# Attention with a feed-forward branch on one core: head quads on four accumulator tiles, blocks taken in linear order, and GpSimd adds over up to three blocks

## The chip, the cores and the metric

The kernel runs on one core of one Trainium2 chip. A core has five engines with an instruction stream of their own each: TensorE (PE in the profile; its weight loads stand apart as PEld), VectorE (DVE), ScalarE (ACT), GpSimd (POOL) and SyncE (SP), which here issues most of the DMAs. The metric is the device time of one execution, in microseconds (us).

## The reference

For 2048 tokens of width 640, the input is normalised once, and two branches of it are added to the input: attention with 32 query heads of width 20 over a single key and value head, and a feed-forward network of width 1728 with a SiLU.

```python
def _A_ref(x, wq, wk, wv, wo):
    q = (x @ wq).reshape(B, S, H, Dh).transpose(0, 2, 1, 3)
    k = x @ wk
    v = x @ wv
    scores = jnp.einsum("bhqd,bkd->bhqk", q, k) * (Dh ** -0.5)
    p = softmax(scores, axis=-1)
    o = jnp.einsum("bhqk,bkd->bhqd", p, v)
    return o.transpose(0, 2, 1, 3).reshape(B, S, H * Dh) @ wo
def _B_ref(x, w1, w2):
    return jnp.einsum("bsf,fd->bsd", silu(jnp.einsum("bsd,df->bsf", x, w1)), w2)
xn = layernorm(x)
return x + _A_ref(xn, wq, wk, wv, wo) + _B_ref(xn, w1, w2)
```

## The kernel before

**Blocks, steps, groups.** The queries are cut into 4 chunks of 512, the keys into 16 tiles of 128. A *unit* is one head of one chunk, so there are 128. A *block* is one unit against one key tile: a score tile of 128 keys by 512 queries, one PSUM bank. There are 2048 blocks. Units are taken three at a time: 42 groups of three heads and one of two. A group runs over the 16 key tiles, and one key tile of one group is a *step*: 43 x 16 = 688 steps. A step computes its blocks' scores with one matmul each (L776, 32 rows of keys by 128 columns, three side by side in different row tiles of TensorE) into three of six banks; consecutive steps alternate between the two halves.

**Two kinds of exp.** ScalarE takes the exp of the step's first two blocks in one instruction of 1024 elements per partition (L794), or of all three (1536). In most steps the last block goes to VectorE instead: it clamps the scores to 16-bit integers (L808, array Z), whose bits, read as bf16, are a coarse exp. To make it finer, such a block is read three times with different offsets and scaled values: as it is (Z), with 43 added (Y, index 0) and with 86 added (Y, index 1). The first sum is made by VectorE for up to three blocks in one instruction (L878, 1536 elements), in `flush_z`; the second by GpSimd for one block in one instruction (L814, two 16-bit numbers handled as one 32-bit integer, so 256 elements), in `do_S`. `want_dve` says which steps give a block to VectorE: not the first 8, not the first step of a group (`KT_ACT`), not the last step of all, and none when the planner's estimate of VectorE's backlog is above 3.4 us (`DVE_TH`).

**The accumulator.** One PSUM bank, number 6, holds the products with the values (PV, L866, weights of 128 by 32). It has four column tiles of 32 partitions. The group's three heads have tiles 0, 1 and 2, with the normaliser as column 20 of the values. The second reading of a VectorE block goes to tile 3; the third goes wherever a tile is free, if need be split over the spare columns of tiles 0 and 1 (the "thirds", `emit_thirds`, `host`, and the instruction group named PT). PV instructions keep the order of their steps (`pv_wait`, `pv_q`); four matmuls in four tiles run side by side and form a *slot*. At a group's end (`end_group`) VectorE copies the bank to SBUF (L986), SP transposes it by DMA (L943), GpSimd puts the parts together in four instructions (L953, L956, L958), VectorE takes a reciprocal (L963), and GpSimd multiplies (L972). The next group's PV starts once the bank is copied.

**Other work.** Between scores and PV, PE takes *jobs* from the queue `misc`: projections of queries (L1064), the feed-forward matmuls (L1100 in, with a tanh on ScalarE at L1113 and a product on VectorE at L1118; L1168 out) and the attention's output matmuls (L1173). `fill_chunk` spreads each chunk's jobs over its steps. Small matmuls on zeros (L699, L712, "fill") occupy PE when the planner finds nothing to do.

**What sets the order.** The program is planned before it is built: `Sched.run` simulates the five engines with given durations and puts out a fixed order of instructions for each. `step` chooses for PE among the next scores, the next PV and a job. On the chip every engine keeps its order and waits on semaphores. The exp blocks live in a ring of 31 (E), the VectorE blocks in 4 sets of 3 (Z and Y).

**Before the first scores** the input is normalised and transposed, and keys and values are made; `PRO` is the order of that on PE. When group 0 ends, `late_loads` issues on SP the loads of w2 and wo and a 1 MB fill of the second query buffer, and on GpSimd five scalings of wo.

The lines on which blocks go to VectorE and when the first sum is made:

```python
if t < DVE_FROM or t % KT >= KT - NOD or t >= self.T - DVE_LAST or t % KT in KT_ACT:
    return False
...
if self.zblocks and (len(self.zblocks) >= (ZB if g < self.NG - 2 else 2) or t - self.zblocks[0][0] >= ZWAIT
                     or t == self.T - 1 or (kt == KT - 1 and g >= FLUSH_G)):
    self.flush_z()
```

Of the kernel before, what the change touches and what calls it, by code (L numbers as in the profile page):

```python
# [10 lines left out]
I32 = mybir.dt.int32  # L11
# [40 lines left out]
H0_STEP = 10  # L52
KT_ACT = (0,)
Y_POOL = True
Y_TIME = 0.72
Y_LOCK = False
# [8 lines left out]
PV_PRESS = 12  # L65
# [9 lines left out]
FLUSH_G = 0  # L75
NOD = 0
PV_HOLD = 11
# [6 lines left out]
PRO = "v0 t7 t8 v1 k2 k3 k4 q1 v2 d0 k5 k6 k7 v3"  # L84
# [6 lines left out]
class Op:  # L91
    __slots__ = ("eng", "dur", "fn", "deps", "prio", "seq", "end", "avail", "idx", "inc", "inc_no", "sem",
                 "on_sched", "name", "dma", "mode", "start", "mm", "work", "kt", "na", "rs", "re", "rl", "then", "after", "lock")

    def __init__(self, eng, dur, fn, deps, prio=0.0, name="", on_sched=None, mode=None):
        self.eng = eng
        self.dur = dur
        self.fn = fn
        self.deps = deps
        self.prio = prio  # L100
        self.name = name
        self.on_sched = on_sched
        self.mode = mode
        self.start = None
        self.end = None
        self.avail = None
        self.idx = None
        self.inc = False
        self.inc_no = None
        self.sem = None  # L110
        self.dma = False
        self.mm = 1
        self.work = dur
        self.then = None
        self.lock = False

# [5 lines left out]
class Sched:  # L122
# [139 lines left out]
    def emit(self):  # L262
        per = {e: [] for e in self.engs}
        for e in self.engs:
            seen = {}
            for op in self.order[e]:
                need = {}
                dm = {}
                for d in op.deps:
                    if d.dma:  # L270
# [90 lines left out]
class Builder:  # L361
# [17 lines left out]
    def alloc(self):  # L379
# [9 lines left out]
        self.v = sb([P, 5, KT, SLOT], BF16)  # L389
# [6 lines left out]
        self.stk = sb([P, 64], BF16)  # L396
        self.UT = sb([P, 2, 4, P], BF16)
        self.W = sb([P, 4, 3, DH + 1], F32)
# [4 lines left out]
        self.tb = sb([P, 2, QW], BF16)  # L403
        self.xres = sb([P, 4, D], BF16)
# [13 lines left out]
        self.rL = sb([P, 2, 4, 3], F32)  # L418
# [3 lines left out]
        self.c86 = sb([P, 1], I32)  # L422
# [28 lines left out]
    def steps_init(self):  # L451
        self.groups = []
        u = 0
        while u < NUNITS:
            self.groups.append(list(range(u, min(u + 3, NUNITS))))
            u += 3
        self.NG = len(self.groups)
        self.T = self.NG * KT
        self.s_next = 0
        self.pv_q = deque()  # L460
        self.pv_wait = deque()
        self.misc = deque()
        self.urgent = deque()
# [6 lines left out]
        self.group_dve = defaultdict(int)  # L470
        self.last_dve_kt = {}
        self.dve_steps = 0
        self.started = False
        self.pv_started = False
        self.u_open = False
# [4 lines left out]
        self.thirds = []  # L480
# [6 lines left out]
        self.first_step = {}  # L487
        for g, us in enumerate(self.groups):
            for x in us:
                self.first_step.setdefault(x // H, g * KT)  # L490
        self.first_step[QC] = self.T


    def more(self):
        return (self.s_next < self.T or bool(self.pv_q) or bool(self.misc) or bool(self.urgent)
                or self.cur_job is not None)
# [43 lines left out]
    def s_reads(self, t, dv):  # L540
        g, kt = divmod(t, KT)
        k = [("kT1" if dv else "kT", kt // 2), ("kT", kt // 2)]
        for x in self.groups[g]:
            k += self.qkeys(x // H, x % H)
            k.append(("qb", (x // H) % 2, x % H))
        return k
# [7 lines left out]
    def s_ready(self, t):  # L554
# [5 lines left out]
        nh = len(self.groups[t // KT])  # L560
# [10 lines left out]
    def step(self, now):  # L571
# [15 lines left out]
        pv_n = 0  # L587
        pv_r = INF
        for op in list(self.pv_q)[:4]:
            if not self.pv_started and not self.may_start_pv():  # L590
                break
            r = sc.ready(op)
            if op.kt < KT:
                r = max(r, self.reads_ready([("vv", op.kt // 2)]))
            if r <= now + 1e-9:
                pv_n += 1
            else:
                if pv_n == 0:
                    pv_r = r
                break  # L600
# [3 lines left out]
        if job is None:  # L604
            for q in (self.urgent, self.misc):
# [7 lines left out]
        used = sum(o.na for o in self.pv_q) + sum(o.na for o, _ in self.pv_wait)  # L613
        press = used > NBLK - PV_PRESS
        choice = None
        if pv_n and (self.pe_mode == "PV" or press or self.pv_q[0].mode == "M"):
# [3 lines left out]
        elif pv_n >= 2:  # L620
# [6 lines left out]
        if self.s_next >= self.T - LASTPV and pv_n:  # L627
            choice = "PV"
        if choice is None:
            return self.fill(now, min(nxt, limit)) or nxt  # L630
        if choice == "PV":
            head = self.pv_q[0]
            d = (0.216 if head.mode == "PV" else head.dur) + self.switch(head.mode)
# [4 lines left out]
        if choice == "PV":  # L638
            op = self.pv_q.popleft()
            if op.kt < KT:  # L640
                op.deps.add(sc.lastw[("vv", op.kt // 2)])
            op.dur = d
            op.work = min(op.work, 0.216)
            self.u_open = op.kt < KT - 1
            self.pe_mode = op.mode
            if op.kt == 0:
                self.u_last = []
            if op.kt == KT:
                self.u_last = op.after
            if op.kt == KT - 1 and getattr(op, "rl", None) is not None:  # L650
                self.u_last = [op.rl]
            if not self.pv_started:
                self.pv_started = True
                op.deps |= sc.deps_of((), [("B", UBANK)])
            sc.commit(op, now)
# [19 lines left out]
    def fill(self, now, until):  # L675
        if self.s_next >= self.T and not self.pv_q:
# [48 lines left out]
    def may_start_pv(self):  # L725
# [5 lines left out]
        return not self.pro_left or len(self.pv_q) >= PV_HOLD  # L731
# [14 lines left out]

    def want_dve(self, t):
        if t < DVE_FROM or t % KT >= KT - NOD or t >= self.T - DVE_LAST or t % KT in KT_ACT:
# [8 lines left out]
    def do_S(self, t, now):  # L757
        sc = self.sc
        g, kt = divmod(t, KT)
        us = self.groups[g]  # L760
        nh = len(us)
# [8 lines left out]
        def fn(pe):  # L770
            ins = None
            for j, x in enumerate(us):
                h = x % H
                r = (h % 4) * SLOT
                kk = 1 if (dv and j == nh - 1) else 0
                ins = pe.matmul(self.bk(par3 + j), self.kT[r:r + SLOT, kk, kt * P:(kt + 1) * P],  # L776
                                self.qT[r:r + SLOT, h // 4, (x // H) % 2, :],
# [20 lines left out]
        zs = zp = None  # L798
        gd = self.group_dve[g]
        if dv:  # L800
            self.dve_steps += 1
            self.group_dve[g] += 1
            self.last_dve_kt[g] = kt
# [7 lines left out]
            self.y_on_pool = Y_POOL  # L811
            if self.y_on_pool:
                c86 = bass.AP(self.c86, self.c86[:, :].offset, [list(self.c86[:, :].ap[0]), [0, QW // 2]])
                sc.new("pool", Y_TIME, lambda v: v.tensor_tensor(  # L814
                    self.Y[:, zs, 1, zp * QW:(zp + 1) * QW].bitcast(I32),
                    self.Z[:, zs, zp * QW:(zp + 1) * QW].bitcast(I32), c86, ALU.add),
                    [("Z", zs, zp), ("c86",)], [("Y", zs, 1, zp)], prio=4.0, name="yp").lock = Y_LOCK
        first = kt == 0
        last = kt == KT - 1

        if dv:
            y = self.Y[:, zs, 0, zp * QW:(zp + 1) * QW].bitcast(BF16)
            z = self.Z[:, zs, zp * QW:(zp + 1) * QW].bitcast(BF16)
        thirds = []

        def pfn(pe):
            ins = None
            for j in range(na):
                q = j if j < nh - 1 else 2
                ins = self.pv_mm(pe, q, 0, kt, self.E[:, (b0 + j) * QW:(b0 + j + 1) * QW], first, last)  # L830
            if dv:
                self.pv_mm(pe, 2, 0, kt, z, first, last)
                ins = self.pv_mm(pe, 3, 1, kt, y, gd == 0, False)
            if first and nh == 2:
                ins = self.pv_mm(pe, 1, 0, kt, self.zero[:, 0:QW], True, False)
            for x in thirds:
                ins = x(pe, 3)
            return ins
        pv = sc.new("pe", 0.3, pfn, [("E", b0 + j) for j in range(na)], [("UB",)],
                    name=f"PV{t}", mode="PV", queue=False)  # L840
        pv.after = None if dv or nh < 3 or gd == 0 else thirds
        pv.mm = na + (2 if dv else 0) + (1 if first and nh == 2 else 0)
        pv.kt = kt
        self.pv_last = pv
        pv.na = na
        self.pv_wait.append((pv, dv))
        if self.thirds and self.can_host(pv):
            self.host(pv, self.thirds.pop(0))
        if dv:
            self.zblocks.append((t, pv))  # L850
        if self.zblocks and (len(self.zblocks) >= (ZB if g < self.NG - 2 else 2) or t - self.zblocks[0][0] >= ZWAIT
                             or t == self.T - 1 or (kt == KT - 1 and g >= FLUSH_G)):
            self.flush_z()
        elif last and self.thirds:
            self.emit_thirds([], None)
        self.move_pv()
        if last:
            self.end_group(g)

    def move_pv(self):  # L860
        waiting = set(id(p) for _, p in self.zblocks)
# [818 lines left out]
```

## Time and profile before

| | |
|---|---|
| median of 3 runs | 734.99 us (733.94 to 735.64) |
| span of the profiled execution (first to last instruction) | 732.1 us |
| granted TensorE clock | 0.997 |
| L794, exps of ScalarE | 688: 625 of 1024, 49 of 1536, 14 of 512 elements |
| L808, blocks of VectorE | 637, mean 684 ns |
| L878, first sums on VectorE | 218, mean 608 ns |
| L814, second sums on GpSimd | 637, mean 692 ns (least 602, median 611, most 1001) |
| L776, score matmuls | 2048 |
| L866, PV matmuls | 3534 |
| L986, evacuations of the accumulator | 43, mean 682 ns |
| first exp, last exp start | 16.9 us, 709.0 us |

The span is what the trace holds; the page gives no other time for the profiled execution, and the median of the runs lies 2.9 us above the span. The mean of an instruction is its own duration. Neighbours on one engine overlap, so what an instruction costs its engine is the distance from its start to the next start.

### The profile page before, as it was taken

The numbers are of one execution on the slowest core, as the hardware profiler recorded it, in microseconds if no ns is written. First come the engines' busy times: TensorE is split into PE (matmuls) and PEld (weight loads), VectorE is DVE, ScalarE is ACT, GpSimd is POOL, SyncE is SP. The second block draws the span as 40 slices with busy tenths as digits, with TensorE's granted clock in tenths as the row PEclk, the third lists the DMA queues.
The fourth block names the chain that finished last, engine by engine and source line by source line (L and its number), as shares of the span: only waits on it lengthen the run. The fifth ranks groups of instructions, "written<-read, shape, count | busy, mean of one in ns | idle before, by whom it ended". The sixth has DMA issues, their size and how long they took to land.

```text
span 732.1 us, 18886 instructions
## 1 busy us (share of the span) xinstructions
PE 714.9 (98%) x6863; PEld 229.2 (31%) x6863; DVE 652.6 (89%) x1189; ACT 695.8 (95%) x780; POOL 524.8 (72%) x897
## 2 busy tenths in 40 slices
PE   8898999999999999999999999999999999999998
PEld 4432222223333233222333233222233322322335
DVE  7788898998998999999899999999989899999883
ACT  6999999999999999999999999999999999999960
POOL 4376877677787777777777777767778877776770
PEclk9999999999999999999999999999999999999999
DMA  9546000000003011000102011110002001200011
GB/s 273 148 123 190 15 17 17 21 15 17 23 9 44 9 52 52 21 18 17 9 8 52 9 26 46 40 19 23 14 8 45 9 9 34 62 9 8 9 38 37
DMA packets 58546, 29.22 MB, mean 40 GB/s; under 512 B 44406, under 2 KB 57814, under 8 KB 58454
## 3 DMA queue, kind: packets, MB, share of 16 engines
q1 hardware_dynamic: 56998, 27.79, 15.1%
q8 instruction: 56, 0.92, 0.6%
q10 hardware_dynamic: 1456, 0.22, 0.2%
q14 instruction: 36, 0.29, 0.1%
HBM read 11.44 MB, written 2.62 MB: 19 GB/s over the span
## 4 chain that ended last, share of the span: by engine, by line
PE 70%; ACT 20%; issue 5%; DVE 4%; DMA 1%; POOL 1%; DVEq 0%; ACTq 0%; POOLq 0%
PE psall L866 23%; PE psall L776 22%; ACT sbt L794 18%; PE psall L1168 8%; PE psall L1100 7%; PE psall L1173 2%; PE psall L1064 2%; PE psall L712 2%; ACT sbt L1113 1%; DVE sbt L808 1%; PE psall L699 1%; DMA sbt<-sbt 1%; DVE sbt L1118 1%; ACT sbt L1458 1%; DVE sbt L1438 0%
## 5 line engine op out<-in xcount | busy, mean ns | idle before, releaser
L794 ACT ACTIVATE sbt<-psall 128x1024 bf16<-128x1024 f32 (+2 forms) x688 | 661.9, 1110 | 9.2 <-PE psall L776 7.7
L814 POOL TENSOR_TENSOR sbt<-sbt 128x256 int32<-128x256 int32 x637 | 436.8, 692 | 158.6 <-DVE sbt L808 143.9
L808 DVE TENSOR_SCALAR sbt<-psall 128x512 int16<-128x512 f32 x637 | 425.9, 684 | 48.2 <-PE psall L776 43.3
L776 PE MATMUL psall<-sbt 32*128 32x512 bf16 x2048 | 269.6, 385 | 6.4 <-ACT sbt L794 3.3
L866 PE MATMUL psall<-sbt 128*32 128x512 bf16 x3534 | 269.2, 385 | 2.1 <-POOL sbt L814 2.1
L776 PEld LDWEIGHTS psall<-sbt 32*128 32x128 bf16 x2048 | 69.2, 91 | 246.8 <-ACT sbt L794 81.1
L878 DVE TENSOR_SCALAR sbt<-sbt 128x1536 int16<-128x1536 int16 (+1 forms) x218 | 132.0, 608 | 2.0
L866 PEld LDWEIGHTS psall<-sbt 128*32 128x32 bf16 x3534 | 66.8, 94 | 113.7 <-issue 77.6
L1168 PE MATMUL psall<-sbt 128*128 128x320 bf16 x448 | 85.4, 302 | 0.2 <-DVE sbt L1118 0.2
L1100 PE MATMUL psall<-sbt 128*128 128x512 bf16 x260 | 79.9, 384 | 2.2 <-DVE sbt L1118 1.9
L1168 PEld LDWEIGHTS psall<-sbt 128*128 128x128 bf16 x448 | 34.7, 97 | 43.7 <-issue 33.1
L1118 DVE SCALAR_TENSOR_TENSOR sbt<-sbt,psall 128x512 bf16<-128x512 bf16 x54 | 36.8, 682 | 2.3 <-ACT sbt L1113 0.7
L1113 ACT ACTIVATE sbt<-psall 128x512 bf16<-128x512 f32 x54 | 37.1, 687 | 0.0
L986 DVE CAST sbt<-psall 128x512 bf16<-128x512 f32 x43 | 29.3, 682 | 1.7 <-PE psall L866 1.6
L1100 PEld LDWEIGHTS psall<-sbt 128*128 128x128 bf16 x260 | 17.8, 97 | 40.7 <-issue 25.8
L1064 PE MATMUL psall<-sbt 128*128 128x512 bf16 (+1 forms) x95 | 29.2, 385 | 0.4 <-DVE sbt L1118 0.4
L1173 PE MATMUL psall<-sbt 128*128 128x320 bf16 x144 | 29.0, 303 | 0.5 <-issue 0.4
L972 POOL TENSOR_TENSOR sbt<-sbt 128x240 bf16<-128x240 f32 (+2 forms) x44 | 25.4, 578 | 2.3 <-DMA sbt<-sbt 1.4
L958 POOL TENSOR_TENSOR sbt<-sbt 128x44 f32<-128x44 f32 x84 | 26.0, 309 | 1.1
L956 POOL CAST sbt<-sbt 128x168 f32<-128x168 bf16 x42 | 14.1, 335 | 9.0 <-DMA sbt<-sbt 9.0
L712 PE MATMUL psall<-sbt 128*128 128x512 bf16 (+1 forms) x70 | 17.4, 403 | 1.9 <-POOL sbt L1368 1.5
L1185 DVE SCALAR_TENSOR_TENSOR sbt<-psall,sbt 128x320 bf16<-128x320 f32 x28 | 13.6, 486 | 6.1 <-PE psall L1168 5.9
(88 smaller groups left out, 207.9 us busy)
## 6 DMA issues: line engine op xcount, KB each, us to landing
sbt<-in_A_x_dram SPq DMA_DIRECT2D x32, 160.0 KB, 3.3
out_dram<-sbt SPq DMA_DIRECT2D x15, 160.0 KB, 1.8
sbt<-in_B_w_dram SPq DMA_DIRECT2D x5, 432.0 KB, 6.6
sbt<-sbt SPq DMA_DIRECT2D x105, 20.0 KB
sbt<-in_B_w_dram SPq DMA_DIRECT2D x13, 160.0 KB, 2.9
sbt<-sbt SPq DMA_TRANSPOSE x68, 2.4
sbt<-sbt SPq DMA_DIRECT2D x1, 1024.0 KB, 6.1
sbt<-in_A_wo_dram SPq DMA_DIRECT2D x5, 160.0 KB, 2.7
```

The lines of the kernel that those rows point to most:

```text
L776: ins = pe.matmul(self.bk(par3 + j), self.kT[r:r + SLOT, kk, kt * P:(kt + 1) * P], self.qT[r:r + SLOT, h // 4, (x // H) % 2, :], start=Tru ...
L794: return a.activation(self.E[:, b0 * QW:(b0 + na) * QW], self.ps[:, par3 * BANK:(par3 + na) * BANK], AF.Exp, scale=ACT_SCALE)
L808: return v.tensor_scalar(self.Z[:, zs, zp * QW:(zp + 1) * QW], self.bk(bb), 0.0, ZMAX, ALU.max, ALU.min)
L814: sc.new("pool", Y_TIME, lambda v: v.tensor_tensor(self.Y[:, zs, 1, zp * QW:(zp + 1) * QW].bitcast(I32), self.Z[:, zs, zp * QW:(zp + 1) * ...
L866: return pe.matmul(self.bk(UBANK, 0, QW, q * SLOT, (q + 1) * SLOT), self.v[:, w, kt, :], x, start=start, stop=stop, tile_position=(0, q * ...
L878: sc.new("dve", Y_SLOW + t_dve_4x(w), lambda v, k=k: v.tensor_scalar(self.Y[:, zs, k, 0:n * QW], Z, float(PH[k + 1][0]), None, ALU.add), z ...
L1064: return pe.matmul(self.bk(b, 0, QW, 0, rows), self.wq[:, k, lo:hi], self.xnT[:, k, c * QW:(c + 1) * QW], start=(k == 0), stop=(k == DC - 1))
L1100: return pe.matmul(self.bk(b), self.w1[:, k, fk * P:(fk + 1) * P], self.xnT[:, k, c * QW:(c + 1) * QW], start=(k == 0), stop=(k == DC - 1))
L1113: sc.new("act", t_act(QW), lambda a: a.activation(t, src, AF.Tanh, scale=0.5), [("B", b)], [("tb", tp)], prio=X_PRIO, name=f"th{c}_{fk}")
L1118: sc.new("dve", t_dve_ps(QW), lambda v: v.scalar_tensor_tensor(out=self.hT[0:rows, fk, :], in0=t, scalar=1.0, in1=src, op0=ALU.add, op1=AL ...
L1168: return pe.matmul(self.bk(b, 0, 320), self.hT[r0:r1, fk, i * P:(i + 1) * P], self.w2[r0:r1, fk, e0:e0 + 320], start=(m == 0), stop=(m == ...
L1173: return pe.matmul(self.bk(b, 0, 320), self.oT[:, k, i * P:(i + 1) * P], self.wo[:, k, e0:e0 + 320], start=(m == 0 and src != "ps"), stop= ...
```

## The change

**Quads in linear order.** Groups are four heads of one chunk (32 groups). A group's 64 blocks are ordered by key tile, then head, and the 2048 blocks follow one another in one line; a step takes the next three, across key tiles and groups, so there are 683 steps, the last with two blocks.

**Head tiles.** Each head has its own column tile, and all three readings of a VectorE block are added there; the thirds and their splitting go, with the spare value columns and the merging on GpSimd. A reading is now an *item* in a queue of its group and tile (`tq`), and `do_pv` starts a slot with the first ready item of each of the four tiles. `pv_ready` counts how many full slots are ready; PV is chosen at `PV_GO` = 5, or with fewer if there is no job.

**GpSimd's adds** move from `do_S` to `flush_z`: one instruction over up to three blocks. The first sum may also be made there by GpSimd, when the planner finds that engine's queue shorter by a margin. **VectorE's steps**: excluded are the first 8, the last, and steps whose last block is one of the last two of its group; the rule on the first step of a group is gone. **Group end**: the DMA transpose takes all 128 rows, VectorE a reciprocal and GpSimd one product of 320 elements. The last group is transposed by four matmuls as a job and multiplied on VectorE.

**Prologue and constants**: `PRO` in another order and a queue of its own (`pro`), `H0_STEP` 14 for 10, `PV_PRESS` 8 for 12, `PV_HOLD` 29 exp blocks for 11 PV instructions; the query offset has its own tile (`qo`), and query jobs read the key `qz` (the fill of the query buffer).

```diff
-H0_STEP = 10
-KT_ACT = (0,)
-Y_TIME = 0.72
+H0_STEP = 14
-PV_PRESS = 12
+PV_PRESS = 8
-PV_HOLD = 11
+PV_HOLD = 29
-PRO = "v0 t7 t8 v1 k2 k3 k4 q1 v2 d0 k5 k6 k7 v3"
+NODB = 2
+GB = 4 * KT
+NB = NUNITS * KT
+Y0_POOL = 1.0
+Y0_COST = 1.45
+YP_FIX = 0.14
+YP_BLK = 0.47
+PV_MIN = 4
+PV_GO = 5
+PRO = "v0 t7 t8 v1 k2 k3 k4 k5 v2 k6 k7 v3 q1 d0"
...
+    def blocks(self, t):
+        return [(b // GB, b % GB // 4, b % 4) for b in range(3 * t, min(3 * t + 3, NB))]
...
+    def pv_ready(self, now):
+        if self.cg >= self.NG or (not self.pv_started and not self.may_start_pv()):
+            return 0, 0, INF
+        g = self.cg
+        closed = self.g_seen[g] == GB and not self.g_late[g]
+        most = max(len(q) for q in self.tq[g])
+        full, some, nxt = 99, 0, INF
+        for q in self.tq[g]:
+            n = 0
+            for it in q[:8]:
+                r = max(self.sc.ready(it), self.reads_ready([("vv", it.kt // 2)]))
+                if r <= now + 1e-9:
+                    n += 1
+                elif r < nxt:
+                    nxt = r
+            some += n > 0
+            if not closed or len(q) == most:
+                full = min(full, n)
+        if not self.sc_bank_free(now):
+            return 0, 0, nxt
+        return full, some, nxt
...
+    def do_pv(self, now, d):
...
+        for q in self.tq[g]:
+            for it in q[:8]:
+                if max(sc.ready(it), self.reads_ready([("vv", it.kt // 2)])) <= now + 1e-9:
+                    items.append(it)
+                    q.remove(it)
+                    break
...
     def want_dve(self, t):
-        if t < DVE_FROM or t % KT >= KT - NOD or t >= self.T - DVE_LAST or t % KT in KT_ACT:
+        g, kt, j = self.blocks(t)[-1]
+        if t < DVE_FROM or 4 * kt + j >= GB - NODB or t >= self.T - DVE_LAST:
             return False
...
+        if self.zblocks and (len(self.zblocks) >= ZB or t - self.zblocks[0][0] >= ZWAIT or t == self.T - 1
+                             or 3 * (t + 1) >= GB * (self.zblocks[0][1] + 1)):
             self.flush_z()
...
+        back = {e: max(sc.t[e], sc.t["pe"]) + sum(o.dur for o in sc.pend[e]) for e in ("dve", "pool")}
+        tp = YP_FIX + YP_BLK * n
+        td = Y_SLOW + t_dve_4x(w)
+        y0 = "pool" if back["pool"] + tp * Y0_COST < back["dve"] + td + Y0_POOL else "dve"
+        for k, e in ((0, y0), (1, "pool")):
+            yk = [("Y", zs, k, i) for i in range(n)]
+            if e == "dve":
+                sc.new("dve", td, lambda v, k=k: v.tensor_scalar(
+                    self.Y[:, zs, k, 0:w], self.Z[:, zs, 0:w], float(PH[k + 1][0]), None, ALU.add), zk, yk,
+                    prio=4.0, name=f"y{k}").lock = True
+                continue
+            c = self.cy[:, k:k + 1]
+            cb = bass.AP(self.cy, c.offset, [list(c.ap[0]), [0, w // 2]])
+            sc.new("pool", tp, lambda v, k=k, cb=cb: v.tensor_tensor(
+                self.Y[:, zs, k, 0:w].bitcast(I32), self.Z[:, zs, 0:w].bitcast(I32), cb, ALU.add), zk + [("cy",)], yk,
+                prio=4.0, name=f"yp{k}")
+        for i, (t, g, kt, j) in enumerate(self.zblocks):
+            for k in range(2):
+                self.item(g, j, kt, k + 1, lambda k=k, i=i: self.Y[:, zs, k, i * QW:(i + 1) * QW].bitcast(BF16),
+                          [("Y", zs, k, i)])
+            self.g_late[g] -= 1
...
+        op = sc.new(eng, 0.75 if eng == "pool" else t_dve_ps(16 * DH), lambda v: v.tensor_tensor(
+            dst, ut[:, :, :, 0:DH], rb, ALU.mult), [key, ("rL", up)], [("o", h0 + i) for i in range(4)],
+            prio=0.5 if eng == "pool" else U_PRIO, name=f"nrm{g}")
...
-        reads = [("xnT", 4 * c + i) for i in range(4)] + [("wqd", 0), ("wqd", 1)]
+        reads = [("xnT", 4 * c + i) for i in range(4)] + [("wqd", 0), ("wqd", 1), ("qz", c % 2)]
```

## The prediction

> **What bounds the kernel now.** I read the page's shares first, then its chain, then busy time by stage, then the groups by shape, and last the order of time on ScalarE and TensorE.
>
> ```profile
> span 732.1 us, 18886 instructions
> ...
> PE 714.9 (98%) x6863; PEld 229.2 (31%) x6863; DVE 652.6 (89%) x1189; ACT 695.8 (95%) x780; POOL 524.8 (72%) x897
> ...
> PE 70%; ACT 20%; issue 5%; DVE 4%; DMA 1%; POOL 1%; DVEq 0%; ACTq 0%; POOLq 0%
> ```
>
> Two engines look full, and the chain changes between them. The busy time by stage (columns: length, PE, PEld, DVE, ACT, POOL, clock, DMA share, GB/s) says which is full where:
>
> ```profile
> 16.86:38.00 21.14, 18.08 (x172) 9.00 (x170) 16.41 (x63) 20.46 (x22) 8.60 (x14) 1.00 0.65 172
> 200.00:400.00 200.00, 199.23 (x1977) 61.62 (x1973) 183.96 (x319) 199.57 (x218) 153.22 (x257) 1.00 0.12 25
> 695.90:710.00 14.10, 13.38 (x129) 3.92 (x126) 14.10 (x27) 10.62 (x17) 12.28 (x21) 1.00 0.23 49
> 710.00:732.10 22.10, 18.71 (x143) 11.36 (x141) 8.12 (x19) 1.60 (x5) 1.48 (x3) 0.99 0.09 30
> ```
>
> From the first exp at 16.86 to 695.9 ACT is never idle for long. In the last group, of two heads, it is idle for 3.5 of 14.1 us. In the tail PE works off output matmuls.
>
> ```profile
> L794 ACT ACTIVATE sbt<-psall 128x1024 bf16<-128x1024 f32 x625 | 594.5, 1090 | 4.9 <-PE psall L776 3.7 <-PE psall L866 0.4 <-ACT sbt L794 0.2
> L814 POOL TENSOR_TENSOR sbt<-sbt 128x256 int32<-128x256 int32 x637 | 436.8, 692 | 158.6 <-DVE sbt L808 143.9 <-PE psall L776 4.3 <-PE psall L866 2.1
> L878 DVE TENSOR_SCALAR sbt<-sbt 128x1536 int16<-128x1536 int16 x202 | 123.8, 614 | 1.9
> L794 ACT ACTIVATE sbt<-psall 128x1536 bf16<-128x1536 f32 x49 | 73.4, 1506 | 0.8 <-PE psall L776 0.8
> L972 POOL TENSOR_TENSOR sbt<-sbt 128x240 bf16<-128x240 f32 x40 | 23.9, 597 | 0.9 <-DVE sbt L963 0.6
> L953 POOL TENSOR_TENSOR sbt<-sbt 128x84 f32<-128x84 bf16 x42 | 15.1, 360 | 0.0
> L794 ACT ACTIVATE sbt<-psall 128x512 bf16<-128x512 f32 x14 | 8.3, 598 | 3.5 <-PE psall L776 3.2
> ```
>
> A mean of one (1090 ns) is not what an exp costs, because neighbours overlap. The cost is from start to start:
>
> ```profile
> 21.78 2.78 ACT L794 ACTIVATE sbt<-psall 128x1536 bf16<-128x1536 f32 x2
> 24.44 0.55 ACT L1412 ACTIVATE sbt<-sbt 128x400 bf16<-128x400 bf16 x1
> ...
> 310.27 3.81 ACT L794 ACTIVATE sbt<-psall 128x1024 bf16<-128x1024 f32 x4
> 313.88 0.69 ACT L1113 ACTIVATE sbt<-psall 128x512 bf16<-128x512 f32 x1
> 314.36 7.05 ACT L794 ACTIVATE sbt<-psall 128x1024 bf16<-128x1024 f32 x7
> ```
>
> So two blocks cost (313.88 - 310.27)/4 = 0.9025 us, three cost (24.44 - 21.78)/2 = 1.33, one of 512 costs 0.48. TensorE the same way:
>
> ```profile
> 309.33 0.39 PE L776 MATMUL psall<-sbt 32*128 32x512 bf16 x3
> 309.65 0.61 PE L866 MATMUL psall<-sbt 128*32 128x512 bf16 x8
> 310.20 0.39 PE L776 MATMUL psall<-sbt 32*128 32x512 bf16 x3
> ...
> 72.44 0.40 PE L866 MATMUL psall<-sbt 128*32 128x512 bf16 x4 [2.06 <-POOL sbt L814]
> ...
> 73.55 1.02 ACT L794 ACTIVATE sbt<-psall 128x1024 bf16<-128x1024 f32 x1 [2.04 <-PE psall L776]
> ```
>
> From the scores at 309.33 to the next PV at 309.65 are 0.32 us, and two PV slots reach the next scores at 310.20, 0.55 later: a slot takes about 0.22 and a change of kind 0.10 more. The pair at 72.44 and 73.55 shows the danger: when a PV at the head of PE's queue waits for a POOL add, ACT loses the same 2 us. Over the whole trace PV waited for that add only 16 times, 7.7 us.
>
> **The change, part by part.**
>
> *ScalarE's exps.* Before, 637 of 688 steps gave their last block to VectorE. The other 51 are the 43 first steps of a group, 7 more among the first 8, and the last; the backlog rule (3.4 us) never bit. Afterwards there are 2048/3 = 683 steps, and the excluded ones are the first 8, the last, and those whose last block is the 63rd or 64th of its 64 (21): 30. So 653 exps of two blocks, 29 of three, and the last step's two.
> Before: 625 x 0.9025 + 49 x 1.33 + 14 x 0.48 = 564.1 + 65.2 + 6.7 = 636.0.
> After: 654 x 0.9025 + 29 x 1.33 = 590.2 + 38.6 = 628.8. **-7.2 us**, on the engine that sets the pace. Each time the backlog rule bites costs 0.43 back.
>
> *The group of two heads* goes. Its idle 3.5 us (10.62 busy of 14.10) goes with it, since the last steps are now like the others: **-3.5**, if PE keeps up; 0 if not.
>
> *TensorE.* Five steps fewer: 5 x 0.32 = -1.6. PV: the starts of L866 cluster into 902 slots for 3534 matmuls. Afterwards each block gives one reading and each VectorE block two more, 2048 + 2 x 653 = 3354; by the rule of which tile gets the VectorE block, the fullest tile of each quad has 22 to 28, in sum 870 slots. That is 32 x 0.216 = -6.9 if every slot is full, and nothing if the planner starts slots half empty. I take half: PE needs some 5 us less where ACT needs 10.7 less. PE's room for the difference shows as fill matmuls, 47 on L699, about 10 us. I book **+1.5** for what PE can't follow (0 to +5).
>
> *GpSimd's adds.* 637 adds of one block become 221 of two or three (211 and 10, by the flush rule). No row shows 768 elements. From below: the rows of 84 and 240 elements rise by (597 - 360)/156 = 1.52 ns per element, so 692 + 512 x 1.52 = 1.47 us. From above: nothing saved, 3 x 692 = 2.08. Nearest is the same operation on 256, less the start of two, which those rows put at 360 - 84 x 1.52 = 0.23: 2.08 - 0.46 = 1.6. So 221 x 1.6 = 354 against 437.
> The Trainium skill (GPSIMD Engine Reference, section 3.1, Elementwise) says that a two-input operation costs about 2.6 cycles per element whatever its length, so that joining adds saves only their starts; an estimate from it, 768 x 2.6/1.2 GHz, is 1.66 us before the start, and by it the sum would be the same but the margin below thinner.
> Normalising: four rows (335, 360, 309 twice, and the 597) over 42 groups, 80 us, become 31 products of 320 elements, 0.597 + 80 x 0.00152 = 0.72 each: 22. POOL falls to 525 - 83 - 58 = 384, and takes those first-phase adds that the planner moves over from VectorE, 0 to 221 of 1.6 us; the rule sends one only where POOL's queue is the shorter, so I take a third, 74: about 500. It stays under the others.
>
> *VectorE.* 16 more reads of scores (426/637 = 0.67 each: +11), 11 fewer evacuations (0.68: -7.5), 74 fewer three-block adds (0.61: -45): about 611 of 653. Nothing on the path.
>
> *Handover of the accumulator.* PV of the next quad waits for the evacuation on VectorE, and behind it waits all later PV; scores and projections go on. One handover costs PV 2.3 us now (last PV ends at 302.57, next starts at 304.87). Afterwards there are 31 in place of 42, each up to 1 us longer, as the last add comes later (1.6 for 0.6): 31 x 3.3 = 102 against 42 x 2.3 = 97. Even. Its cover is the buffer of 31 exp blocks: a pause of 3.3 us fills about 7; without it, ACT would stand for 31 x 1 us.
>
> *Moved loads.* The end of group 0 moves from step 16 to step 22, some 6 us. With it, on SP's queue, go the transpose, 15 loads of w2 (8.5 us of issue from 50.78), 5 of wo, the 1 MB fill of the second query buffer, and on POOL the five scalings of wo (785 ns each). First users: the output matmuls at 166, and the second chunk's projections, which now wait for that fill ahead of PE's other jobs; they are paced past step 50. Nothing, unless such a job stands at the head early. The prologue's new order: ACT is busy 20.46 of 21.14 us there, so at best -0.7; I take 0, at worst +2.
>
> *Tail.* The last VectorE blocks' add is of two or three, so the last PV starts later by up to 1.6 - 0.6; the four transposing matmuls and the product of 320 in place of two of 80 add 0.1. PE has output matmuls to do meanwhile (it was busy 18.7 of 22.1), so I take **+1.0** (0 to +1.5).
>
> Sum: -7.2 - 3.5 + 1.5 + 1.0 = -8.2: a span of 723.9. The median of the runs, 734.99, lies 2.9 above this span; kept, that gives **727 us**, with 723 to 732 for this case.
>
> **The rivals.**
> 1. *PE follows less.* If slots go half empty, so that 902 stay, PE needs only 1.6 less; in the last chunk, where output matmuls are left over, that is what shows: 735 - 1.6 = **733**. For it: PE 98%, chain 70% PE. Against: fills exist, so PE had room.
> 2. *The adds come late (slower).* The planner counts 0.14 + 0.47 per block, 1.55 us for three; that is a number in the diff, not a measurement. If one really takes 2.08, each set is 0.53 late, and PE's order is fixed. If a quarter of the 221 is met at the head of PE's queue, 55 x 0.53 = 29 us; the room of 10 takes its part, 19 remain: 735 - 8.2 + 19 = **746**. For it: 72.44, and that the mean add, 692, lies above the median, 611, so POOL is already held up at times. Against: only 7.7 us of such waits now, though then with 0.72 planned for 0.69. It decides from 8.2 + 10 = 18.2 us, 0.33 in each of 55: at adds over 1.88 us.
> 3. *ACT gains all.* PE's room suffices and the tail hides its add: -10.7, and up to 4 more where 11 fewer handovers spare small waits of 0.3: **720 to 724**.
>
> **How the numbers follow.** Forecast 0.52; PE short 0.13; late adds 0.24; all gained 0.11. About 0.2% (1.5 us) is what a measurement of this kernel can tell from no change. Faster: 0.11, nearly all of 0.52, and a little of the PE case: 0.65. Same: 0.07, from the PE case. Slower: 0.24 and edges of the others: 0.28. The range 716 to 748 goes below the all-gained case by what its small waits may give, and above the late case's middle; some 0.15 stay outside.
>
> **What would show it.** Right: 653 exps of two blocks and 29 of three at the same spacing; ACT idle under 1 us per 100; last exp near 701; PV in some 870 to 890 slots; the three-block add near 1.6; the tail still 22 to 23. Wrong: PE's waits on POOL's adds above 20 us; more than 35 exps of three blocks (the backlog rule bites); the add above 1.9 us; POOL busier than 85%; or more output matmuls left after the last exp than now.

## The result and the profile after

The changed kernel takes 739.43 us (median of 4 runs, 738.85 to 740.91) against 735.07; the ratio is 1.0067, with a 95% interval of 1.005 to 1.0083. It is slower by 4.4 us where 8 us less were forecast. The profiled execution is the longest of the four, 740.91 us, 2.0 above its span.

From the page of the changed kernel, its shares and its chain:

```profile
span 738.9 us, 17791 instructions
...
PE 709.2 (96%) x6661; PEld 223.8 (30%) x6661; DVE 659.1 (89%) x1106; ACT 695.0 (94%) x775; POOL 489.8 (66%) x366
...
PE 58%; DVE 19%; issue 11%; POOL 8%; ACT 3%; DMA 0%; POOLq 0%; DVEq 0%
```

The chain is the work that ended last, followed back from the end. Before the change VectorE's share of it was 4%, GpSimd's 1% and "issue" (no wait that the profile shows) 5%; why issue rose to 11% is open. The span is longer, but ScalarE is busy for a smaller part of it (695.8 of 732.1 us before, now 695.0 of 738.9). The groups by shape (count, then busy us, mean ns, then idle time before them with what ended it) show what was counted rightly and what was not:

```profile
L841 ACT ACTIVATE sbt<-psall 128x1024 bf16<-128x1024 f32 x654 | 620.9, 1053 | 19.0 <-PE psall L823 15.9 <-ACT sbt L841 0.4
L856 DVE TENSOR_SCALAR sbt<-psall 128x512 int16<-128x512 f32 x653 | 433.2, 682 | 49.0 <-PE psall L823 41.5 <-POOL sbt L888 0.9
L888 POOL TENSOR_TENSOR sbt<-sbt 128x768 int32<-128x768 int32 x280 | 432.9, 1563 | 198.9 <-DVE sbt L856 155.3 <-PE psall L823 26.4 <-issue 4.1
L882 DVE TENSOR_SCALAR sbt<-sbt 128x1536 int16<-128x1536 int16 x142 | 123.8, 872 | 2.5
L841 ACT ACTIVATE sbt<-psall 128x1536 bf16<-128x1536 f32 x29 | 42.0, 1466 | 0.6 <-PE psall L823 0.5
```

The exps are the 653 + 1 and 29 that the rule gives. The joined GpSimd add takes 1.563 us. But VectorE's first sum on three blocks (now L882), the same instruction with the same shape as before, takes 872 ns in the mean, and took 614. VectorE stood idle for only 2.5 us before all 142 of them: the added time is inside the instruction.

The waits say who felt it. Before (waiter, awaited, us in total, times, longest):

```profile
PEld psall L776 <- DVE sbt L808: 45.2, 114, 1.0
...
ACT sbt L794 <- PE psall L776: 7.7, 15, 2.0
...
PEld psall L866 <- POOL sbt L814: 5.6, 15, 2.4
```

After:

```profile
PEld psall L823 <- DVE sbt L856: 71.2, 162, 1.2
...
ACT sbt L841 <- PE psall L823: 16.3, 35, 1.5
...
PEld psall L762 <- POOL sbt L888: 13.3, 43, 0.8
```

Scores (L823, in these rows by their weight loads, PEld) wait for a bank that VectorE has not read yet, 26 us more, and ScalarE waits for scores. The waits of PV (L762) on GpSimd grew as well, but only by 8 us.

**Where 6.8 us of span came from.** First exp at 18.0 in place of 16.9: +1.2. From the first exp's start to the last one's lie 692.2 us before and 701.6 after: +9.4; the exps need 7.2 less, so ScalarE's waits grew by 16.6 (3.8 of them before 60 us: idle 4.9 of 42.0 us there, 1.1 of 43.1 before). After the last exp's start 23.1 us remained, now 19.3: -3.8, since 42 feed-forward output matmuls are left over by then and 65 were before (23 x 0.136 us = 3.1); PE had had time for them while scores waited. Together 1.2 + 9.4 - 3.8 = 6.8.

**The clock is a small part.** The granted TensorE clock was 0.88 between 18.02 and 60 us and 1.00 in the same stage before. Over the span it was 0.992 (0.995 in the other three runs), before 0.997. An estimate from these: 0.005 of 738.9 us, some 4 us of TensorE's time at most in the profiled execution, and some 1.5 in the others.

The order of time shows one of the longest of ScalarE's waits, on four engines:

```profile
554.99 4.31 POOL L888 TENSOR_TENSOR sbt<-sbt 128x768 int32<-128x768 int32 x3 [0.95 <-PE psall L823]
...
558.02 1.69 DVE L882 TENSOR_SCALAR sbt<-sbt 128x1536 int16<-128x1536 int16 x1
...
560.04 1.95 DVE L856 TENSOR_SCALAR sbt<-psall 128x512 int16<-128x512 f32 x3
...
560.86 0.39 PE L823 MATMUL psall<-sbt 32*128 32x512 bf16 x3 [0.99 <-DVE sbt L856]
...
561.29 1.94 ACT L841 ACTIVATE sbt<-psall 128x1024 bf16<-128x1024 f32 x2 [1.54 <-PE psall L823]
```

GpSimd's adds run until 559.30. VectorE's sum starts at 558.02 and ends at 559.71, 0.41 after them. Behind it come one other VectorE instruction (0.48 us) and, at 560.04, the clamp of the next block; TensorE stands idle for 0.99 before the next scores, and ScalarE for 1.54. Sorted over the whole trace: VectorE's three-block sums that start while no GpSimd add runs take 563 ns in the mean (53 of them), those that start during one, at least 0.06 us before its end, 1056 (89). Before it was 558 (107) and 677 (95). Of the 89, 85 end 0.41 to 0.46 us after the very add that they met, and before 87 of the 95 did. So a sum that meets a GpSimd add stands until that ends, and an unhindered GpSimd add is now 1.46 us long where it was 0.61.

### The profile page after: what moved, and what is told of

Its sections match the earlier page's. It is cut to its first block, busy times and chain, and to the rows that moved or that the text cites. A ratio compares the mean times of both kernels' runs of the same rounds, so it can differ in the third digit from the quotient of the medians.

```text
span 738.9 us, 17791 instructions
## 1 busy us (share of the span) xinstructions
PE 709.2 (96%) x6661; PEld 223.8 (30%) x6661; DVE 659.1 (89%) x1106; ACT 695.0 (94%) x775; POOL 489.8 (66%) x366
## 4 chain that ended last, share of the span: by engine, by line
PE 58%; DVE 19%; issue 11%; POOL 8%; ACT 3%; DMA 0%; POOLq 0%; DVEq 0%
PE psall L823 19%; PE psall L762 18%; DVE sbt L856 11%; PE psall L1081 9%; POOL sbt L888 8%; PE psall L1013 5%; DVE sbt L882 5%; PE psall L977 2%; PE psall L684 2%; PE psall L1086 1%; ACT sbt L841 1%; DVE sbt L1031 1%; ACT sbt L1362 1%; DVE sbt L931 1%; DVE sbt L1116 1%
## 5 line engine op out<-in xcount | busy, mean ns | idle before, releaser
L841 ACT ACTIVATE sbt<-psall 128x1024 bf16<-128x1024 f32 (+1 forms) x683 | 658.1, 1071 | 19.7 <-PE psall L823 16.3
L888 POOL TENSOR_TENSOR sbt<-sbt 128x768 int32<-128x768 int32 (+1 forms) x292 | 446.6, 1546 | 202.2 <-DVE sbt L856 158.6
L856 DVE TENSOR_SCALAR sbt<-psall 128x512 int16<-128x512 f32 x653 | 433.2, 682 | 49.0 <-PE psall L823 41.5
L823 PE MATMUL psall<-sbt 32*128 32x512 bf16 x2048 | 268.2, 386 | 15.9 <-DVE sbt L856 10.9
L762 PE MATMUL psall<-sbt 128*32 128x512 bf16 x3354 | 263.8, 386 | 4.6 <-DVE sbt L931 2.3
L823 PEld LDWEIGHTS psall<-sbt 32*128 32x128 bf16 x2048 | 68.2, 91 | 255.6 <-issue 98.0
L882 DVE TENSOR_SCALAR sbt<-sbt 128x1536 int16<-128x1536 int16 (+1 forms) x150 | 131.5, 876 | 2.7
L762 PEld LDWEIGHTS psall<-sbt 128*32 128x32 bf16 x3354 | 65.0, 94 | 119.4 <-issue 76.0
L977 PE MATMUL psall<-sbt 128*128 128x512 bf16 (+1 forms) x95 | 28.9, 385 | 0.6 <-DVE sbt L1031 0.6
L920 POOL TENSOR_TENSOR sbt<-sbt 128x320 bf16<-128x320 bf16 x31 | 26.8, 865 | 3.8 <-DVE sbt L915 3.4
L931 DVE CAST sbt<-psall 128x512 bf16<-128x512 f32 x32 | 21.8, 680 | 2.1 <-PE psall L762 2.1
L684 PE MATMUL psall<-sbt 128*128 128x512 bf16 (+2 forms) x76 | 20.3, 420 | 1.5 <-POOL sbt L1281 1.5
L1482 POOL TENSOR_SCALAR sbt<-sbt 128x256 bf16<-128x256 bf16 x8 | 4.1, 514 | 23.4 <-DVE sbt L1480 23.3
L1098 DVE SCALAR_TENSOR_TENSOR sbt<-psall,sbt 128x320 bf16<-128x320 f32 x28 | 13.5, 484 | 4.6 <-PE psall L1081 4.2
L1116 DVE SCALAR_TENSOR_TENSOR sbt<-psall,sbt 128x320 bf16<-128x320 f32 x28 | 13.2, 480 | 3.1 <-PE psall L1086 3.1
```

The costliest lines, as they stand in the source:

```text
L684: return pe.matmul(self.bk(b, 0, n), self.zero[:, 0:P], self.zero[:, 0:n], start=True, stop=True)
L762: ins = pe.matmul(self.bk(UBANK, 0, QW, r, r + SLOT), self.v[:, it.w, it.kt, :], it.x(), start=f, stop=False, tile_position=(0, r), skip_g ...
L823: ins = pe.matmul(self.bk(par3 + i), self.kT[r:r + SLOT, kk, kt * P:(kt + 1) * P], self.qT[r:r + SLOT, g % 8, (g // 8) % 2, :], start=True ...
L841: return a.activation(self.E[:, b0 * QW:(b0 + na) * QW], self.ps[:, par3 * BANK:(par3 + na) * BANK], AF.Exp, scale=ACT_SCALE)
L856: return v.tensor_scalar(self.Z[:, zs, zp * QW:(zp + 1) * QW], self.bk(bb), 0.0, ZMAX, ALU.max, ALU.min)
L882: sc.new("dve", td, lambda v, k=k: v.tensor_scalar(self.Y[:, zs, k, 0:w], self.Z[:, zs, 0:w], float(PH[k + 1][0]), None, ALU.add), zk, yk, ...
```

## The experiments

Theory A is this hold. Rival B is the prediction's second rival, PV waiting for late GpSimd adds. Rival C is the other prologue and its clock. Times are medians; each ratio is against the kernel before on the same chip, whose medians lay at 734.2 to 734.4 (735.07 for the result above). Differences between two changed kernels are of their medians and so compare chips too.

**Short adds under the same plan.** In `flush_z`, the add's instruction is issued once per block. The planner's durations are untouched, so every engine keeps its order:

```diff
-            sc.new("pool", tp, lambda v, k=k, cb=cb: v.tensor_tensor(
-                self.Y[:, zs, k, 0:w].bitcast(I32), self.Z[:, zs, 0:w].bitcast(I32), cb, ALU.add), ...
...
+            def padd(v, k=k, c1=c1):
+                for i in range(n):
+                    ins = v.tensor_tensor(
+                        self.Y[:, zs, k, i * QW:(i + 1) * QW].bitcast(I32),
+                        self.Z[:, zs, i * QW:(i + 1) * QW].bitcast(I32), c1, ALU.add)
+                return ins
+            sc.new("pool", tp, padd, zk + [("cy",)], yk, prio=4.0, name=f"yp{k}")
```

> The changed kernel with each GpSimd add over two or three blocks issued as two or three adds of one block (256 elements each) in the place of one; the planned order is the same on every engine. Theory A (VectorE's three-block add stands still until the GpSimd add under way has ended, and a GpSimd add is now 1.46 us long where it was 0.61): VectorE's add, mean 872 ns in the changed kernel, falls to 600 to 720; ScalarE's waits between exps fall from some 40 us towards 25; the time falls by 5 to 12 us, to 728 to 735. Rival B (PV waits for late GpSimd adds): three single adds take some 1.75 us where the plan counts 1.55, so PV comes later still, PE's waits on GpSimd rise above 13 us and the time rises by 3 to 8 us, to 742 to 748. Rival C (the other prologue order and its clock): no change within 1.5 us.

Measured: 732.12 us, ratio 0.997 (0.9959 to 0.9981), 7.3 below the changed kernel (6.6 with each taken against the kernel before on its own chip). At the same granted clock, 0.995, it is 733.26 against 738.85 to 739.93. Its groups, and then one of its waits:

```profile
L892 POOL TENSOR_TENSOR sbt<-sbt 128x256 int32<-128x256 int32 x864 | 543.7, 662 | 104.6 <-DVE sbt L856 76.7 <-PE psall L823 16.1 <-issue 6.7
L882 DVE TENSOR_SCALAR sbt<-sbt 128x1536 int16<-128x1536 int16 x142 | 96.1, 677 | 2.5
```

```profile
PEld psall L762 <- POOL sbt L892: 29.7, 64, 1.0
```

GpSimd is busy for some 97 us longer with its adds, PV waits for them more than twice as long, and the kernel is faster: VectorE's sum fell from 872 to 677 ns. That speaks for A and against B. And 91 of the 101 sums that met an add ended 0.41 to 0.46 us after that one add, though a set has two or three adds: the length of the instruction sets the hold, not that of the set. ScalarE's waits did not fall to 25 us, but to 31.6, counted as what the starts of neighbouring exps lie apart beyond 0.9025 us for two blocks and 1.33 for three (40.9 in the changed kernel, 23.8 before). The -7.3 us is a net figure: PE's waits for the adds rose beside it, from 14 to 38 us.

**One part alone: joined adds in the kernel before.** The add moves from `do_S` to `flush_z`; all else is as it was (only the new instruction is shown).

```diff
...
+        sc.new("pool", 0.14 + 0.47 * n, lambda v: v.tensor_tensor(
+            self.Y[:, zs, 1, 0:w].bitcast(I32), self.Z[:, zs, 0:w].bitcast(I32), c86, ALU.add),
+            zk + [("c86",)], [("Y", zs, 1, i) for i in range(n)], prio=4.0, name="yp")
```

> The kernel before with one part of the change alone: GpSimd's second sum over up to three blocks in one add, issued when the set is complete. Theory A: VectorE's add, mean 614 ns before, rises to 750 to 900, and the time rises by 4 to 12 us, to 739 to 747. Rival B: GpSimd's add becomes later by up to 1.6 us, PE's waits on it rise from 8 us to 20 or more and the time rises by as much, with VectorE's add unchanged. Rival C (what costs is elsewhere in the change): within 2 us of 735.

Measured: 770.72 us, ratio 1.0495 (1.0473 to 1.0518): 36 us, far above the range of A.

```profile
L876 POOL TENSOR_TENSOR sbt<-sbt 128x768 int32<-128x768 int32 x202 | 323.6, 1602 | 232.3 <-DVE sbt L808 194.9 <-PE psall L776 15.3 <-issue 8.4
L872 DVE TENSOR_SCALAR sbt<-sbt 128x1536 int16<-128x1536 int16 x202 | 180.2, 894 | 2.1
```

VectorE's sum rose from 614 to 894 ns, as A has it, while PE's waits on this add stayed near 9 us. Here all 218 sums are VectorE's, so 202 x 0.28 = 57 us more fall on an engine that was 89% busy. The held sums also reach PV, which A's range left out: PE waited 22.6 us for them ahead of PV, 2.1 in the kernel before.

**The first sum always on VectorE** (`y0 = "dve"`; none of the 71 shifts).

> The changed kernel with the first sum always on VectorE (none of the 71 shifts to GpSimd). Theory A: 221 VectorE adds in place of 150, while GpSimd is busy some 110 us less and so meets fewer of them; VectorE gains 71 x 0.65 = 46 us of work less the holds spared, and the mean of its add falls below 800 ns. If holding costs most, the time stays within 3 us of the changed kernel's 739.4; if VectorE's load as such limits, it rises to 745 or more. Rival B: fewer GpSimd adds, so PV waits less and the time falls by 3 to 6 us.

Measured: 754.5 us, ratio 1.0273. The mean sum was 831 ns, not below 800 as A had it, and 211 of them were due. By the alternative stated ahead, VectorE's load as such limits, and the holds are a part of that load. The shift to GpSimd is worth 15 us in the changed kernel; B's expectation fell again.

**The plan keeps the two apart** (`.lock = True` on GpSimd's adds).

> The changed kernel with GpSimd's adds locked against VectorE's first sums in the plan, as its normalising products already are: the planner starts neither while the other runs. Theory A: VectorE's add falls to about 0.6 us; what the time does depends on whether the plan finds room: if so it falls by 4 to 10 us (729 to 735), if both engines then queue, it rises by up to 10. Rival B: adds come later in the plan, PV waits are planned, time up by 0 to 5 us. Rival C: no change.

Measured: 733.7 us, ratio 0.9993 (0.9981 to 1.0006), within A's range. VectorE's sum takes 736 ns in the mean, not the expected 600: 31 sums still met an add, and 89 did without a lock, so a plan can avoid most meetings but not all.

**The prologue's order as before** (`PRO` and `H0_STEP` taken back).

> The changed kernel with the prologue's order and the first job's step as before (k5 to k7 after q1 and d0; step 10). Theory A: the early loss (step 64 starts 80.4 us after the first exp, against 76.7 before) comes from the held adds; the time stays within 2 us of 739.4. Rival C: the prologue's order costs 2 to 4 us; the time falls to 735 to 737.

Measured: 746.04 us, ratio 1.0164: 6.6 us slower than the changed kernel. Rival C has the wrong sign; the new order helps. A's expectation, within 2 us, failed too. One wait is as long as the whole difference: ScalarE stands for 7.0 us until 47.95, while scores wait for keys that are still being made. Step 64 starts 87.0 us after the first exp, in the changed kernel 80.4, with short adds 75.7.

**Short adds, and a plan that knows their duration** (`0.04 + 0.6 * n` for `tp` in the operation; the rule of the shift keeps its numbers).

> As the split adds (one-block GpSimd adds, time 732.1), but the plan counts 0.04 + 0.6 us per block, 1.84 for three, as they took, in the place of 1.55. Theory A2 (what is left of the loss with split adds is PV placed too early: PE waited 38 us on GpSimd's adds): PE's waits on them fall below 15 us and the time by 3 to 6 us, to 726 to 729. Rival: those waits lie beside other work, and the time stays within 1.5 us of 732.

Measured: **722.33 us**, ratio 0.9844 (0.9824 to 0.9863), faster than both kernels, below the expected range. A group of this run, and then three of its waits:

```profile
L882 DVE TENSOR_SCALAR sbt<-sbt 128x1536 int16<-128x1536 int16 x161 | 108.1, 672 | 2.7
```

```profile
PEld psall L823 <- DVE sbt L856: 57.7, 144, 0.8
PEld psall L762 <- POOL sbt L892: 6.8, 23, 0.7
ACT sbt L841 <- PE psall L823: 4.6, 10, 1.0
```

PE's waits on the adds fell as expected (38 us with the short plan, now 7.3). ScalarE's waits by its starts are 19.9 us, less than before the change.

**That plan, with joined adds.** Only the instruction differs from the last kernel; the plan counts 1.84 us where a joined add takes 1.5.

> The planned order of the split-add kernel with true durations (722.3) on every engine, but each GpSimd add over two or three blocks is again one instruction, as in the changed kernel: two kernels that differ in the length of a GpSimd instruction alone, under a plan that counts more than either takes. Theory A (the hold): VectorE's add rises from 672 to 850 or more and the time by 6 to 14 us, to 728 to 736. Rival (the planned duration was what mattered, not the hold): joined adds are shorter in sum, so 718 to 724.

Measured: 746.16 us, ratio 1.0161: 23.8 us above its twin. At the same granted clock, 0.995, it is 744.82 and 746.05 against 724.5. PV's waits on GpSimd are as short as there (6.2 us); what differs is this, two groups and then two waits:

```profile
L888 POOL TENSOR_TENSOR sbt<-sbt 128x768 int32<-128x768 int32 x261 | 410.6, 1586 | 223.7 <-DVE sbt L856 170.9 <-PE psall L823 29.3 <-PE psall L762 9.0
L882 DVE TENSOR_SCALAR sbt<-sbt 128x1536 int16<-128x1536 int16 x161 | 133.2, 828 | 2.7
```

```profile
PEld psall L823 <- DVE sbt L856: 80.6, 169, 1.6
ACT sbt L841 <- PE psall L823: 19.9, 46, 1.2
```

The sum's mean is a little below the expected 850, the time above the expected 736. VectorE's 161 sums are 25 us longer in total (133.2 against 108.1), and here no gain for PV stands against it. The planned duration alone is refuted as a cause.

**Joined adds, the plan told of the hold** (VectorE's sum counted 0.3 us longer).

> The changed kernel with one-instruction adds, its plan told of the hold: VectorE's first sum counts 0.3 us more (0.865 for three blocks, where 0.872 was measured). If the loss was the plan's ignorance, the time falls by 5 to 12 us, to 727 to 734; if VectorE has no room for the holds even when planned, it falls by less than 3.

Measured: 740.84 us, ratio 1.0087. Telling the plan of a longer sum does not help; the sum took 972 ns this time. That speaks for the holds themselves as the cost, and against the plan's ignorance of their mean.

**Three more plans with short adds.** Both locked apart and short:

> As the kernel just described (split adds with their true durations in the plan), and GpSimd's adds locked in the plan against VectorE's first sums. If holds of VectorE still cost something at one-block adds (mean 677 ns against 560 alone), its mean falls below 620 and the time by 1 to 4 us against that kernel; if locking costs more room than it spares, the time rises by 2 to 8 us.

Measured: 740.57 us, ratio 1.0082, 18 us above the same kernel without the lock, where 2 to 8 were expected at worst; the sum stayed at 691 ns and 35 exps had three blocks: locking costs room. The second sum planned block by block, as before the change:

> The joining undone as the kernel before had it: GpSimd's second sum planned and issued for each block as soon as its scores are clamped (0.64 us in the plan), the first sum as in the kernel with split adds and true durations. Theory A2: the second sums come up to 1.2 us earlier, PV is freer; 724 to 729. Rival: no better than split adds, within 1.5 us of them.

Measured: 723.61 us, ratio 0.9855 (0.9826 to 0.9884), not told apart from 722.33, as its rival had it. VectorE's sum counted 0.1 us longer:

> The split-add kernel with true GpSimd durations (722.3), and VectorE's first sum counted 0.1 us longer (0.665 for three, where 0.672 was measured). If what is left of ScalarE's waits comes from that 0.1, the time falls by 1 to 3 us, to 719 to 721; else it stays within 1.5 us.

Measured: 726.9 us, ratio 0.9894, 4.6 worse though its durations are nearer to what was measured. So two plans can differ by some 5 us for no reason that a mean shows, and the 9.8 us between the two short-add kernels of 732.1 and 722.3 can't be laid to one cause with certainty; nor can the 5.7 us that the lock gained. The two pairs with one plan each, -7.3 and +23.8 us, do not have this doubt.

## Why the prediction was wrong

The sign was wrong; the time lies inside the range, for another reason than the slower rival's.

- *ScalarE's exps*: right, 653 + 1 and 29, -7.2 us of work.
- *The group of two heads*: right. In this window of the changed kernel (length, PE, PEld, DVE, ACT) ScalarE is busy 17.77 of 18 us in the last steps:

```profile
700.00:718.00 18.00, 17.89 (x189) 5.39 (x187) 16.28 (x27) 17.77 (x20) 13.18 (x9) 1.00 0.17 38
```

- *TensorE's slots*: right, 874 clusters of starts for 3354 matmuls, where 870 was the full-slot count, so the first rival's half-empty slots did not come. The handover was easier than thought: from the starts, PV paused 2.2 us at 31 group ends, and 2.6 at 42 before.
- *GpSimd's adds*: right in size. 1.563 us for the predicted 1.6, 71 shifts for 74, 490 us busy for 500.
- *VectorE*: **the step that failed** is "74 fewer three-block adds (0.61: -45): about 611 of 653. Nothing on the path." The count was right, 150 are left. The price was carried over from the row of before, and it is set by the partner: the 150 took 131.5 us, 0.876 each, where some 90 us were booked. VectorE is busy for 659 us in place of the 611 forecast, and some 40 of these lie inside the held sums, in front of the clamp that frees a bank for scores. That put VectorE on the path (19% of the chain). The prediction took "POOL is already held up at times" from 692 against 611 and asked only what this does to GpSimd. The same trace held the other side: 614 in the mean against a median of 560.
- The Trainium skill (SBUF — State Buffer, section SBUF: two separate sides) says that VectorE in a two-port mode and GpSimd share a port pair as an exclusive lock, held for the whole instruction, so that the later one fully blocks. No row of the trace names an instruction's mode; on the hold the runs agree: most held sums end 0.41 to 0.46 us after the GpSimd add that they met, and their mean grew with the length of that add (677 to 1056 ns). Joining three adds is thus a change of the lock's length, and this rule spoke against it.
- *PE follows less* was booked at +1.5; ScalarE's waits grew by 16.6, by the experiments in the main from the hold, at most some 4 from the clock. *Prologue*: booked at 0; the first exp came 1.2 later in this trace, but at 16.5 to 17.9 us in the other runs with the new order. *Tail*: +1.0 booked, -3.8 measured, as PE had leftover work done earlier. The 2.9 us between span and median were too many: executions here lie 1.8 to 2.2 above their span.
- *The rival of late adds*: not what happened. PE waited 14 us on GpSimd, below the 20 that it named, and the kernel in which PE waited most for adds was faster.
- *The signs*: none of the five signs of being wrong appeared, and the forecast failed all the same, since no sign was named for VectorE. Two of the signs of being right failed: the last exp started at 719.6 and not near 701, and ScalarE was idle 1.7 us per 100 between 200 and 400 us, 2.9 between 400 and 600.

With the hold shortened the forecast's own mechanism stands: 732 under the same plan, 722 under one with the adds' true durations, 11.8 us below the kernel before. That it lies near the third rival's 720 to 724 is in part luck: that rival counted joined adds, some hold is left (672 ns against 560), and two plans can differ by 5 us.

## What to carry to other kernels

An instruction's price from a trace holds for the neighbours that it had there. When one engine's instruction is made longer, ask which other engine's instructions slow down while it runs, sort their durations by whether they overlap it, and reprice them by the new length. On a shared resource several short instructions can beat one long one, though their sum is longer.

## What the runs showed of the hardware

- A VectorE sum of 1536 16-bit elements from SBUF to SBUF takes 0.56 us alone. If it starts during a GpSimd add of 256 32-bit elements it takes 0.66 to 0.74 in the mean (where the plan did not lock the two), during one of 768 elements 1.06 to 1.26; the longest took 1.76 in the changed kernel. VectorE's reads of scores from PSUM show nothing of the kind (684 and 682 ns).
- GpSimd's add has a start of about 0.17 us and 1.67 ns per 32-bit element: by least durations 602 ns at 256 and 1458 at 768. Joining three saved 0.35 of 1.81 us.
